# Grouped-query decode attention on one core: a shorter TensorE program with its prologue behind the loop, branch hints, and small ScalarE steps on GpSimd

## The chip, the cores and the metric

One core of a Trainium2 chip: TensorE (matrix products), VectorE, ScalarE, GpSimd, SyncE (which here issues most transfers) and 16 DMA engines that load from HBM into SBUF. The metric is the device time of one execution in microseconds, the median of several runs of the same program.

## The reference

One decode step for a batch of 2: layer norm, grouped-query attention over a cache of 32,768 keys and values for 8 key/value heads (32 query heads, 4 to each key/value head, 128 wide), an output projection, gated by a small two-layer block. Cut to what matters:

```python
xn = layernorm(x)                                   # x: [2, 1, 512]
q = (xn @ wq).reshape(B, 1, 32, 128).transpose(0, 2, 1, 3)
k, v = repeat(k_cache, 4, axis=1), repeat(v_cache, 4, axis=1)   # caches: [2, 8, 32768, 128]
p = softmax(einsum("bhqd,bhkd->bhqk", q, k) * 128 ** -0.5)
s = einsum("bhqk,bhkd->bhqd", p, v).reshape(B, 1, 4096) @ wo
x1 = xn + shifted(gelu(layernorm(xn) @ w1)) @ w2    # with one position, every shift gives zeros
g = silu(x1 + gelu(layernorm(x1) @ w3) @ w4)
out = x + s * g
```

All inputs are bfloat16. The caches are 268 of the 280.5 MB that are read.

## The kernel before

A *group* is one (batch, key/value head) pair; there are 16, each with 8.4 MB of K and 8.4 MB of V. The program is written out engine by engine, ordered by semaphores alone; `Queue` counts an engine's instructions, and `take` waits for a semaphore and lowers it.

- SyncE loads wq, w3, w4 and the first K (L214 to L217), then for each group K (L342) once half of the last group's scores are done (`s_half`), V (L331) once the last P·V is done (`s_pv`), for the last group in halves (L348, L336), and at the end wo in three parts (L354). K has three half-size slots in `kbuf`, V two in `vbuf`; wq lies in K's third slot.
- VectorE (loop at L406, two groups a turn) turns K in 16 blocks into tiles `T` (L416, four buffers), finds the peak of the scores (L399, L401, L426, L428 give `shift`), transposes the exponentials into `pt` (L432), forms row sums (L431) and their reciprocal (L436). Late in the next group it finishes the previous group's head: `on` (L385), `xm` and `oXs` (L389, L393).
- TensorE (loop at L468, a group a turn) makes the scores (L477), the sum of the peaks (L487), the softmax sum (L492, two fp32 products), P·V into four quadrants of `o` (L500); in the middle of the next group `head_oT` (L452, four fp32 products over `ob`) and `head_xp` (L462). After the loop it repeats the two heads for the last group and makes the output product with wo (L518, 128 products).
- ScalarE makes the exponentials (L374), and copies: `z`, the weights of the next group's scores (L360, four pieces), `ob` from `o` (L379), `oX` from `oXs` (L367).
- The prologue makes q (L287, L294) and the gate (L305, L317) while the first K is loading.

Both loops have `head_slot` 0: the loop's first instruction is placed at the start of a block in which the engine fetches its instructions. TensorE's prologue lies ahead of its loop in memory, the output product behind it.

Of the kernel before, what the change touches and what calls it, by code (L numbers as in the profile page):

```python
# [18 lines left out]
VT = 4  # L19
# [44 lines left out]

@with_exitstack
def kernel(
# [55 lines left out]
    rs = [sb(f"rs{i}", [128, 1], F32) for i in range(NPART)]  # L122
    sm = [sb(f"sm{i}", [128, rep], F32) for i in range(NPART)]
# [18 lines left out]
    sel_o = sb("sel_o", [128, VT, rep], F32)  # L142
    sel_h = sb("sel_h", [128, rep], F32)
# [7 lines left out]
    xn_bf = sb("xn_bf", [B, D], BF16)  # L151
    ln2_bf = sb("ln2_bf", [B, D], BF16)
    xT = sb("xT", [128, 2 * DK, B], BF16)
    q_sb = sb("q_sb", [128, B, Hq], BF16)
# [14 lines left out]
    S = bank("S", rep + NPART * 32)  # L169
# [19 lines left out]
    pe = Queue(nc.tensor, sem("s_pe"))  # L189
# [6 lines left out]
    t_d = sem("t_d")  # L196
# [15 lines left out]
    with tc.tile_critical(no_gpsimd_drain=True):  # L212
# [8 lines left out]
        e_x4z = po.op(lambda e: e.memset(x4_bf[:, :], 0.0))  # L221
        e_id0 = po.op(lambda e: e.memset(ident[:, :], 0.0))
# [6 lines left out]
        po.op(lambda e: e.memset(ob[:, :], 0.0), inc=(t_ob, 1))  # L229
# [4 lines left out]
        e_o0 = ve.op(lambda e: e.memset(o[:, :], 0.0))  # L234
        ve.op(lambda e: e.memset(pro[:, :], 0.0))
        e = ve.op(lambda e: e.tensor_copy(out=xf[:, :], in_=x_bf[:, :]), (d_x, 16))
# [15 lines left out]
        e_xnb = ve.op(lambda v: v.tensor_copy(out=xn_bf[:, :], in_=xn[:, :]), e_xn)  # L252
        e = layernorm(ln2, xn, "ln2", e_xn)
        e_lnb = ve.op(lambda v: v.tensor_copy(out=ln2_bf[:, :], in_=ln2[:, :]), e)
        for j in range(4):
# [5 lines left out]
            axis=AX.X, op=ALU.add))  # L261
        e_selh = ve.op(lambda v: v.tensor_reduce(
# [14 lines left out]
        treg = xp_b[:, :].bitcast(BF16)  # L277
        for s, (src, ev) in enumerate(((xn_bf, e_xnb), (ln2_bf, e_lnb))):
            for k in range(DK):
                c = (s * DK + k) * B  # L280
                e = pe.op(lambda t, c=c, src=src, k=k: t.transpose(
                    out=treg[:, c:c + B], in_=src[0:B, k::DK], identity=ident[0:B, 0:B]), ev, e_id)
        e_xT = ve.op(lambda v: v.tensor_copy(out=xT[:, :, :], in_=treg[:, 0:2 * DK * B].rearrange("p (k b) -> p k b", b=B)), e)
        for h in range(Hq):
            for k in range(DK):
                last = h == Hq - 1 and k == DK - 1
                e = pe.op(lambda t, h=h, k=k: t.matmul(  # L287
                    pro[:, h * B:(h + 1) * B], lhsT=wq3[:, k, h * Dh:(h + 1) * Dh], rhs=xT[:, k, :],
                    start=(k == 0), stop=(k == DK - 1)), e_xT, (d_wq, 16), inc=last)
        e_q = ve.op(lambda v: v.tensor_copy(out=q_sb[:, :, :], in_=pro[:, 0:Hq * B].rearrange("p (h b) -> p b h", b=B)), e)  # L290
# [10 lines left out]
        hT = sc[0]  # L301
        for f in range(FK):
            for k in range(DK):
                last = f == FK - 1 and k == DK - 1
                e = pe.op(lambda t, f=f, k=k: t.matmul(  # L305
                    hT[:, f * B:(f + 1) * B], lhsT=w3v[:, k, f::FK], rhs=xT[:, DK + k, :],
                    start=(k == 0), stop=(k == DK - 1)), (d_w3, 16), inc=last)
        e_hf = ve.op(lambda v: v.tensor_copy(out=hf[:, :], in_=hT[:, 0:FK * B]), e)
# [30 lines left out]
        for m in range(1, NG):  # L339
            base = m % 2  # L340
            if m < NG - 1:
                sp.op(lambda e, m=m, base=base: e.dma_start(  # L342
                    out=kbuf[:, base * SLOT:(base + NPART) * SLOT], in_=row_view(A_k_cache, *groups[m])),
                    (s_half, m), e_q, inc=(t_k[0], 16))
                nc.sync.sem_inc(t_k[1], 16)
            else:
                for i, h in enumerate(order(m)):
                    sp.op(lambda e, m=m, h=h, base=base: e.dma_start(  # L348
                        out=kbuf[:, (base + h) * SLOT:(base + h + 1) * SLOT],
                        in_=row_view(A_k_cache, *groups[m])[:, h * SLOT:(h + 1) * SLOT]),  # L350
                        (s_half, m), inc=(t_k[i], 16))
            load_v(m, (s_pv, m))
        for i, (a, c) in enumerate(wo_parts):
            sp.op(lambda e, a=a, c=c: e.dma_start(out=wo3[:, a:c, :], in_=wos[:, a:c, :]), (s_pv, NG - 1), inc=(d_wo[i], 16))  # L354


        def put_z(b, k):
            for j in range(4):
                c = (NR - 1) * rep + 32 * j
                ac.op(lambda v, j=j, c=c: v.copy(  # L360
                    out=z[32 * j:32 * j + 32, :, :, c:c + rep],
                    in_=qr[32 * j:32 * j + 32, :, :, b, k * rep:(k + 1) * rep]),
                    e_qr, e_z0, inc=(t_z, 1) if j == 3 else False)

        def keep_oX(m):
            b, k = groups[m]
            return ac.op(lambda v: v.copy(out=oX[:, k, :, b], in_=oXs[:, :]), (s_oX, m + 2))  # L367

        put_z(*groups[0])
        for m in range(NG):  # L370
            if m:
                keep_oX(m - 1)
            for i in range(NPART):
                ac.op(lambda v, i=i: v.activation(  # L374
                    out=ep[i][:, :], in_=sc[i][:, :], func=ACT.Exp, scale=inv_sqrt_dh, bias=shift[:, :], accum_out=rs[i][:, :]),
                    (s_shift, m + 1), e_tf if m == 0 else None, inc=(t_e, 1))
            if m < NG - 1:
                put_z(*groups[m + 1])
            ac.op(lambda v: v.copy(out=ob[:, :], in_=o[:, :]), (s_pv, m + 1), inc=(t_ob, 1))  # L379
        e_oX = keep_oX(NG - 1)  # L380
# [6 lines left out]
        def head_out():  # L387
# [4 lines left out]
            with nc.allow_low_precision(reason="three of the four terms are zero, the fourth is bf16"):  # L392
                nc.vector.tensor_reduce(out=oXs[:, :], in_=xm[:, :, :], axis=AX.X, op=ALU.add).then_inc(s_oX, 1)  # L393
# [12 lines left out]
        with nc.Fori(0, NG // 2, engines=[DVE], head_slot={DVE: 0}):  # L406
            for par in range(2):
                for i, h in enumerate(order(par)):
# [3 lines left out]
                    for r in range(NR):  # L412
                        n = i * NR + r
                        if n >= T_BUFS:
# [3 lines left out]
                            in_=kt[:, r * W:(r + 1) * W].rearrange("p (t b k) -> p t b k", b=NB, t=RT)).then_inc(t_T, 1)  # L418
                        if i == 1 and r == 3:
# [6 lines left out]
                nc.vector.tensor_reduce(out=top[:, :], in_=S[:, rep:], axis=AX.X, op=ALU.max).then_inc(t_d, 1)  # L426
                take(nc.vector, t_d)
                nc.vector.tensor_scalar_mul(out=shift[:, :], in0=top[:, :], scalar1=-inv_sqrt_dh).then_inc(s_shift, 1)  # L428
                for i, h in enumerate(order(par)):
                    take(nc.vector, t_e)  # L430
                    nc.vector.tensor_scalar_mul(out=sm[i][:, :], in0=sel_h[:, :], scalar1=rs[i][:, 0:1])  # L431
# [4 lines left out]
                nc.vector.reciprocal(out=rec[:, :], in_=S[:, 0:rep]).then_inc(t_oT, 1)  # L436
        head_on()
        head_out()
# [10 lines left out]
        def head_oT(first=None):  # L449
            take(nc.tensor, t_ob)  # L450
            for t in range(VT):
                ins = nc.tensor.matmul(  # L452
                    oT[:, :], lhsT=ob[:, t * Dh:(t + 1) * Dh], rhs=sel_o[:, t, :],
                    start=(t == 0), stop=(t == VT - 1))
                if t == 0 and first is not None:
                    ins.then_inc(first, 1)
            ins.then_inc(t_oT, 1)
# [9 lines left out]
        pe.wait(e_o0, e_ones, e_const, e_hf, e_tf)  # L467
        with nc.Fori(0, NG, engines=[PE], head_slot={PE: 0}):  # L468
            take(nc.tensor, t_z)
            for i in range(NPART):  # L470
                for r in range(NR):
# [3 lines left out]
                    for nb in range(NB):  # L475
                        for w in range(2):
# [3 lines left out]
                                stop=(r == NR - 1 and nb == NB - 1 and w == 1))  # L480
                    ins.then_inc(t_used, 1)
                    if i == 1 and r == 3:
                        head_xp()
                if i == 0:
                    head_oT(s_half)
            take(nc.tensor, t_mx)
            nc.tensor.matmul(  # L487
                S[:, rep:], lhsT=same_h[:, :], rhs=mxr[:, :, :].rearrange("p i r -> p (i r)"),
                start=True, stop=True).then_inc(t_top, 1)
            take(nc.tensor, t_pt, NPART)  # L490
            for i in range(NPART):
                ins = nc.tensor.matmul(S[:, 0:rep], lhsT=ones_f[:, :], rhs=sm[i][:, :], start=(i == 0), stop=(i == NPART - 1))  # L492
            ins.then_inc(t_S, 1)
# [13 lines left out]
        head_oT()  # L507
        head_xp()


        for i, (a, c) in enumerate(wo_parts):
            for k in range(a, c):
                pe.wait(e_s0, e_oX, (d_wo[i], 16))
                for r in range(NQ):
                    gr = k * NQ + r
                    for n in range(NQ):
                        col = r * D + n * QW
                        pe.op(lambda t, k=k, r=r, n=n, col=col, gr=gr: t.matmul(  # L518
                            pro[32 * n:32 * n + B, 0:QW], lhsT=oX[:, k, r, :], rhs=wo3[:, k, col:col + QW],
                            start=(gr == 0), stop=(gr == Hkv * NQ - 1), tile_position=(0, 32 * n)),  # L520
                            inc=(gr == Hkv * NQ - 1 and n == NQ - 1))
# [30 lines left out]
```

## Time and profile before

| | us |
|---|---|
| median of 3 runs | 659.79 (659.31 to 660.29) |
| the profiled execution | 659.97 |
| its span, first to last instruction | 657.6 |
| busy: TensorE / VectorE / ScalarE / GpSimd | 413.3 / 372.4 / 53.1 / 2.2 |
| DMA: 280.5 MB at a mean of 427 GB/s, share of 16 engines | 98.7% |

The profile lists, for one execution, each engine's work by source line, what ended its idle time, DMA queues with packets and bytes, and slices or windows of time with the share that 16 DMA engines were busy. A row such as "L416 DVE ... x8 [1.91 <-DVEq L396]" reads: eight instructions of line 416 on VectorE in a row, idle 1.91 us before them, ended by the engine's own queue at line 396 (`take`). Transfers of data are in queue q1 (from SyncE) and q10 (from ScalarE); packets of the kind "instruction" bring the engines' programs.

### The profile page before, as it was taken

The numbers are of one execution on the slowest core, as the hardware profiler recorded it, in microseconds if no ns is written. First come the engines' busy times: TensorE is split into PE (matmuls) and PEld (weight loads), VectorE is DVE, ScalarE is ACT, GpSimd is POOL, SyncE is SP. The second block draws the span as 40 slices with busy tenths as digits, with TensorE's granted clock in tenths as the row PEclk, the third lists the DMA queues.
The fourth block names the chain that finished last, engine by engine and source line by source line (L and its number), as shares of the span: only waits on it lengthen the run. The fifth ranks groups of instructions, "written<-read, shape, count | busy, mean of one in ns | idle before, by whom it ended". The sixth has DMA issues, their size and how long they took to land. (4 is left out here: it accounts for less than half of the span.)

```text
span 657.6 us, 7019 instructions
## 1 busy us (share of the span) xinstructions
PE 413.3 (63%) x2654; PEld 180.6 (27%) x2686; DVE 372.4 (57%) x530; ACT 53.1 (8%) x168; POOL 2.2 (0%) x11
## 2 busy tenths in 40 slices
PE   2528386564838756583865659476574947657965
PEld 2313132231313223131322313132232413213423
DVE  4238193663819367291945729184582918548760
ACT  1110101010010101001010100101010010100010
POOL 1000000000000000000000000000000000000000
PEclk9959787687978769797876979788697977869797
DMA  8999999999999999999999999999999999999995
GB/s 366 432 445 438 443 446 403 438 439 442 442 407 438 438 442 442 419 427 438 442 442 427 423 442 435 442 435 415 442 435 442 438 411 442 438 442 419 419 426 222
DMA packets 6460, 280.61 MB, mean 427 GB/s; under 512 B 682, under 2 KB 692, under 8 KB 1716
## 3 DMA queue, kind: packets, MB, share of 16 engines
q1 hardware_dynamic: 6408, 280.50, 98.7%
q8 instruction: 4, 0.07, 0.0%
q14 instruction: 4, 0.03, 0.0%
q10 hardware_dynamic: 44, 0.01, 0.0%
HBM read 280.50 MB, written 0.00 MB: 427 GB/s over the span
## 5 line engine op out<-in xcount | busy, mean ns | idle before, releaser
L416 DVE STREAM_TRANSPOSE T<-kbuf 128x1024 int32<-128x1024 int32 x256 | 292.8, 1210 | 177.4 <-DVEq L396 177.4
L477 PE MATMUL sc<-T,z 128*128 128x512 bf16 x992 | 270.8, 420 | 146.7 <-PEq L396 142.5
L477 PEld LDWEIGHTS sc<-T,z 128*128 128x128 bf16 x1024 | 99.7, 104 | 304.4 <-issue 221.4
L500 PE MATMUL o<-vbuf,pt 128*16 128x512 bf16 x1024 | 91.1, 535 | 0.0
L492 PE MATMUL S<-sm,ones_f 128*128 128x4 f32 x64 | 15.8, 352 | 53.6 <-PEq L396 53.6
L500 PEld LDWEIGHTS o<-vbuf,pt 128*16 128x16 bf16 x1024 | 30.5, 118 | 52.9 <-issue 45.1
L367 ACT COPY oX<-oXs 128x4 bf16<-128x4 bf16 x16 | 3.1, 196 | 375.8 <-DVE oXs L393 375.8
L399 DVE TENSOR_REDUCE mx<-sc 128x1 f32<-128x512 f32 x32 | 21.5, 672 | 15.7 <-DVEq L396 15.7
L492 PEld LDWEIGHTS S<-sm,ones_f 128*128 128x128 f32 x64 | 14.8, 322 | 55.3 <-issue 55.3
L374 ACT ACTIVATE ep<-sc,shift 128x512 bf16<-128x512 f32 x32 | 21.7, 683 | 77.1 <-DVE shift L428 77.1
L432 DVE STREAM_TRANSPOSE pt<-ep 128x512 bf16<-128x512 bf16 x32 | 22.6, 705 | 0.0
L487 PE MATMUL S<-mxr,same_h 128*128 128x64 f32 x32 | 6.5, 285 | 22.0 <-PEq L396 22.0
L452 PEld LDWEIGHTS oT<-sel_o,ob 128*128 128x128 f32 x136 | 17.7, 191 | 4.0 <-issue 1.3
L379 ACT COPY ob<-o 128x512 f32<-128x512 f32 x16 | 9.4, 586 | 115.0 <-PE o L500 115.0
L452 PE MATMUL oT<-sel_o,ob 128*128 128x4 f32 x136 | 16.2, 242 | 0.8 <-PEq L396 0.8
L431 DVE TENSOR_SCALAR sm<-sel_h,rs 128x4 f32<-128x4 f32 x32 | 6.7, 209 | 15.4 <-DVEq L396 15.4
L436 DVE RECIPROCAL rec<-S 128x4 f32<-128x4 f32 x16 | 2.9, 183 | 20.5 <-DVEq L396 20.5
L487 PEld LDWEIGHTS S<-mxr,same_h 128*128 128x128 f32 x32 | 4.8, 188 | 29.8 <-issue 29.8
L360 ACT COPY z<-qr 32x16 bf16<-32x16 bf16 x64 | 12.6, 197 | 3.9 <-issue 3.3
L401 DVE TENSOR_SCALAR mxr<-row_of,mx 128x32 f32<-128x32 f32 x32 | 7.7, 241 | 4.8 <-DVEq L396 0.3
L426 DVE TENSOR_REDUCE top<-S 128x1 f32<-128x64 f32 x16 | 3.6, 225 | 11.2 <-DVEq L396 11.2
L385 DVE TENSOR_TENSOR on<-oT,rec 128x4 bf16<-128x4 f32 x17 | 2.7, 156 | 7.9 <-DVEq L396 7.9
(73 smaller groups left out, 72.7 us busy)
## 6 DMA issues: line engine op xcount, KB each, us to landing
kbuf<-in_A_k_cache_dram SPq DMA_DIRECT2D x2, 4096.0 KB, 21.9
vbuf<-in_A_v_cache_dram SPq DMA_DIRECT2D x2, 4096.0 KB, 20.4
kbuf<-in_A_wq_dram SPq DMA_DIRECT2D x1, 4096.0 KB, 12.2
vbuf<-in_B_w_dram SPq DMA_DIRECT2D x2, 1792.0 KB, 18.6
kbuf<-in_A_wo_dram SPq DMA_DIRECT2D x1, 2048.0 KB, 29.5
kbuf<-in_A_wo_dram SPq DMA_DIRECT2D x1, 1536.0 KB, 32.8
kbuf<-in_A_wo_dram SPq DMA_DIRECT2D x1, 512.0 KB, 33.5
kbuf<-in_A_k_cache_dram SPq DMA_DIRECT2D x15, 27.6
```

The lines of the kernel that those rows point to most:

```text
L360: ac.op(lambda v, j=j, c=c: v.copy(out=z[32 * j:32 * j + 32, :, :, c:c + rep], in_=qr[32 * j:32 * j + 32, :, :, b, k * rep:(k + 1) * rep]) ...
L374: ac.op(lambda v, i=i: v.activation(out=ep[i][:, :], in_=sc[i][:, :], func=ACT.Exp, scale=inv_sqrt_dh, bias=shift[:, :], accum_out=rs[i][: ...
L379: ac.op(lambda v: v.copy(out=ob[:, :], in_=o[:, :]), (s_pv, m + 1), inc=(t_ob, 1))
L399: nc.vector.tensor_reduce(out=mx[:, i:i + 1], in_=sc[i][:, :], axis=AX.X, op=ALU.max).then_inc(t_d, 1)
L401: ins = nc.vector.tensor_scalar_mul(out=mxr[:, i, :], in0=row_of[:, :], scalar1=mx[:, i:i + 1])
L416: nc.vector.transpose(out=Ts[n % T_BUFS][:, :].rearrange("p (b t k) -> p t b k", b=NB, t=RT), in_=kt[:, r * W:(r + 1) * W].rearrange("p (t ...
L432: nc.vector.transpose(out=pt[h][:, :, :].rearrange("p r (t h) -> p t r h", h=rep), in_=ep[i][:, :].rearrange("p (t r h) -> p t r h", r=NR, ...
L452: ins = nc.tensor.matmul(oT[:, :], lhsT=ob[:, t * Dh:(t + 1) * Dh], rhs=sel_o[:, t, :], start=(t == 0), stop=(t == VT - 1))
L477: ins = nc.tensor.matmul(sc[i][:, :], lhsT=z[:, nb, w, zc:zc + 128], rhs=Tb[:, nb, :, w], start=(r == 0 and nb == 0 and w == 0), stop=(r = ...
L487: nc.tensor.matmul(S[:, rep:], lhsT=same_h[:, :], rhs=mxr[:, :, :].rearrange("p i r -> p (i r)"), start=True, stop=True).then_inc(t_top, 1)
L492: ins = nc.tensor.matmul(S[:, 0:rep], lhsT=ones_f[:, :], rhs=sm[i][:, :], start=(i == 0), stop=(i == NPART - 1))
L500: ins = nc.tensor.matmul(o[32 * j:32 * j + VT * rep, :], lhsT=pt[h][:, r, a * VT * rep:(a + 1) * VT * rep], rhs=vt[:, u * VT:(u + 1) * VT, ...
```

## The change

TensorE's program: the prologue is recorded and placed behind the loop. A register `turn` counts: at 0 the first branch goes to the prologue, at 1 to 16 to a group, then on to the output. The prologue computes q and the gate with xT as the weights and 448 to 512 columns of wq or w3 as the moving side, in four quadrants, and VectorE transposes the results: 32 and 16 products instead of 128 and 56. `head_oT` is one fp32 product instead of four, because VectorE now masks `o` and adds its four quarters (`head_ob`, in place of ScalarE's copy of `o`); the softmax sum is one product of 8 columns, added by VectorE. The output product starts ahead of the last `head_xp`. A branch hint stands ahead of the output product; VectorE's loop has a hint for its back edge instead of `head_slot`. GpSimd makes `z` (one masked product instead of four copies) and copies `oX`; the last `oX` is written by VectorE. SyncE releases `head_ob` with `t_o`, after each V issue.

```diff
-    pe = Queue(nc.tensor, sem("s_pe"))
+    pe = LateQueue(nc.tensor, sem("s_pe"))      # keeps what it is given until place()
...
+        for i in range(NPART):
             for k in range(DK):
+                for n in range(NQ):
+                    e = pe.op(lambda t, i=i, k=k, n=n: t.matmul(
+                        sc[i][32 * n:32 * n + B, :], lhsT=xT[:, k, :],
+                        rhs=wq3[:, k, :].rearrange("p (h n y) -> p h n y", n=NQ, y=32)[:, i * HH:(i + 1) * HH, n, :],
+                        start=(k == 0), stop=(k == DK - 1), tile_position=(0, 32 * n)), ...)
+            e = ve.op(lambda v, i=i: v.transpose(out=qT[:, i * 512:(i + 1) * 512], in_=sc[i][:, :]), e)
...
             load_v(m, (s_pv, m))
+            nc.sync.sem_inc(t_o, 1)
...
+        sp.wait((s_pv, NG))
+        nc.sync.sem_inc(t_o, 1)
...
-        def put_z(b, k):
-            for j in range(4):
-                c = (NR - 1) * rep + 32 * j
-                ac.op(lambda v, j=j, c=c: v.copy(
-                    out=z[32 * j:32 * j + 32, :, :, c:c + rep], ...
+        def put_z(m):
             b, k = groups[m]
+            po.op(lambda v: v.tensor_mul(out=z_cols,
+                in0=qr[:, :, :, b, k * rep:(k + 1) * rep].rearrange(...).broadcast_to([128, 2 * NB, 4, rep]),
+                in1=quad[:, :].unsqueeze(1).unsqueeze(3).broadcast_to([128, 2 * NB, 4, rep])),
+                e_qr, e_z0, e_quad, (s_shift, m) if m else None, inc=(t_z, 1))
...
-            ac.op(lambda v: v.copy(out=ob[:, :], in_=o[:, :]), (s_pv, m + 1), inc=(t_ob, 1))
...
+        def head_ob():
+            take(nc.vector, t_o)
+            nc.vector.tensor_mul(
+                out=ob[:, :].rearrange("p (t d) -> p t d", t=VT), in0=o[:, :].rearrange("p (t d) -> p t d", t=VT),
+                in1=row_t[:, :].unsqueeze(2).broadcast_to([128, VT, Dh])).then_inc(t_d, 1)
+            take(nc.vector, t_d)
+            nc.vector.tensor_reduce(
+                out=obm[:, :], in_=ob[:, :].rearrange("p (t d) -> p d t", t=VT), axis=AX.X, op=ALU.add).then_inc(t_ob, 1)
...
-        with nc.Fori(0, NG // 2, engines=[DVE], head_slot={DVE: 0}):
+        with nc.Fori(0, NG // 2, engines=[DVE], hint_back_edge=True):
...
+                        if i == 0 and r == 3:
+                            head_ob()
...
-            for t in range(VT):
-                ins = nc.tensor.matmul(
-                    oT[:, :], lhsT=ob[:, t * Dh:(t + 1) * Dh], rhs=sel_o[:, t, :],
-                    start=(t == 0), stop=(t == VT - 1))
+            nc.tensor.matmul(oT[:, :], lhsT=obm[:, :], rhs=sel_h[:, :], start=True, stop=True).then_inc(t_oT, 1)
...
-        with nc.Fori(0, NG, engines=[PE], head_slot={PE: 0}):
+        with nc.body("pe_turn", valid_engines=[PE]):
+            nc.br_ne(turn, 0, on_true="pe_groups", on_false="pe_prologue", engines=[PE])
+        with nc.body("pe_groups", valid_engines=[PE]):
...
+            nc.br("pe_next", engines=[PE])
+        with nc.body("pe_output", valid_engines=[PE]):
+            in_next_block = nc.tensor.mark_branch_hint_location()
+            head_oT()
+            for i, (a, c) in enumerate(wo_parts):
+                if i == 1:
+                    nc.tensor.br_ne(turn, 0, "pe_output_2", "pe_turn").branch_hint(in_next_block)
+                    nc.switch_bb("pe_output_2")
+                    head_xp()
...
+        with nc.body("pe_prologue", valid_engines=[PE]):
+            prologue.place()
...
+        with nc.body("pe_next", valid_engines=[PE]):
+            nc.regs_alu(turn, turn, 1, op=ALU.add)
+            nc.br_lt(turn, NG + 1, on_true="pe_turn", on_false="pe_output", engines=[PE])
```

## The prediction

> **What bounds the kernel now.** I read the page's slices first, then its DMA queues.
>
> ```profile
> GB/s 366 432 445 438 443 446 403 438 439 442 442 407 438 438 442 442 419 427 438 442 442 427 423 442 435 442 435 415 442 435 442 438 411 442 438 442 419 419 426 222
> ...
> q1 hardware_dynamic: 6408, 280.50, 98.7%
> q8 instruction: 4, 0.07, 0.0%
> q14 instruction: 4, 0.03, 0.0%
> ```
>
> The 16 DMA engines are busy for 98.7% of the span, so nothing that VectorE or TensorE does in the middle sets the time. The DMA view cut to 80:640 says the same more sharply, and names the one other thing that uses these engines:
>
> ```profile
> q1 hardware_dynamic: 4492, 242.62, 100.0%
> q14 instruction: 1, 0.01, 0.0%
> ```
>
> Instructions come through the same engines. Narrow windows of that view place the q8 packets at 19.1, 35.7 and 74.1 us and, by a window over the end, after 640; each takes its engine 0.9 us (5.0%, 4.9% and 4.6% of 16 engines over 1.2 us). The q14 packets stand at 35.8, 41.5 and 146.9, 0.3 us each. I read q8 as TensorE's: its packets come as TensorE is in the prologue, enters the loop, ends the first turn, and nears the last matmul. Through the next 14 turns there is none.
>
> A lump on one engine is never made up, since every engine always has its next load queued. The windows at the end show it (columns: span, busy us and count by engine, clock, DMA share, GB/s):
>
> ```profile
> 649.00:649.50 0.50, 0.00 (x0) 0.00 (x0) 0.24 (x2) 0.00 (x0) 0.00 (x0) 0.52 0.90 369
> 649.50:650.00 0.50, 0.07 (x6) 0.10 (x10) 0.10 (x1) 0.20 (x1) 0.00 (x0) 0.50 0.32 131
> 650.00:650.50 0.50, 0.50 (x24) 0.50 (x27) 0.00 (x0) 0.00 (x0) 0.00 (x0) 0.50 0.24 98
> 650.50:651.00 0.50, 0.50 (x32) 0.50 (x24) 0.00 (x0) 0.00 (x0) 0.00 (x0) 0.50 0.14 57
> 651.00:651.50 0.50, 0.50 (x32) 0.50 (x24) 0.00 (x0) 0.00 (x0) 0.00 (x0) 0.50 0.04 16
> ```
>
> Most engines finish at 649.5; about four go on, the last to about 651.3. After 649.5 are left (0.32 + 0.24 + 0.14 + 0.04) x 0.5 us x 16 = 5.9 engine-us. Shared evenly they would end 0.4 us later, at 649.9: the stragglers make every load land up to 1.4 us late.
>
> The last group then runs as a chain. Its rows in the timeline, and the chain of waits behind them:
>
> ```profile
> 612.81 9.24 DVE L416 STREAM_TRANSPOSE T<-kbuf 128x1024 int32<-128x1024 int32 x8 [1.91 <-DVEq L396]
> ...
> 616.33 0.59 ACT L379 COPY ob<-o 128x512 f32<-128x512 f32 x1 [7.22 <-PE o L500]
> ...
> 622.62 4.62 DVE L416 STREAM_TRANSPOSE T<-kbuf 128x1024 int32<-128x1024 int32 x4 [0.57 <-DVEq L396]
> ...
> 639.23 0.98 PE L492 MATMUL S<-sm,ones_f 128*128 128x4 f32 x4 [3.35 <-PEq L396]
> ...
> 646.51 0.59 ACT L379 COPY ob<-o 128x512 f32<-128x512 f32 x1 [8.47 <-PE o L500]
> ```
>
> ```profile
> 648.72 0.24 PE xp L462 x4
> 648.96 0.97 issue
> 649.93 3.16 PE pro L518 x126
> 653.09 0.02 issue
> 653.12 0.30 DVE sg L442
> ```
>
> Both halves of the last K make VectorE wait (1.91 and 0.57 us): 622.62 is set by DMA. From there all is compute: P·V ends at 646.45, and 6.64 us of ob, oT, on, xp, oXs, oX and the output product follow, to 653.09.
>
> **The change, part by part.** The sum is made on the profiled execution: 659.97 us, that is a span of 657.6 and 2.4 around it, 0.2 above the median of 659.79.
>
> *Instruction fetches.* Moving the prologue behind the loop puts the loop in the part of the program that is there before the first q8 packet; 299 fewer instructions leave fewer pieces to bring. I count one of TensorE's fetches left in the stream (the start jumps past the loop into the prologue, which brings what lies behind it) out of three, and one of VectorE's two, since it now falls into its loop without a jump; ScalarE loses 96 copies and perhaps its packet at 146.9. The straggler now is about 1.8 us behind 649.5 and carries by its size more than one lump. One lump costs between its own 0.9 us and the 1.4 us that even sharing would save; I take 1.2, by the middle. Gain 1.8 - 1.2 = 0.6. Bounds: 0 (as many lumps as now) and 1.6 (none left: 1.4 and the lumps' own 3.7 engine-us over 16).
>
> By the Trainium skill (Runtime: NRT & Kernel Launch, "Instruction fetch mechanics") a sequencer holds two 16 KiB pieces, and a taken branch to a third stalls for a DMA fetch; the same section gives TensorE 128 KiB. The trace fits the larger figure: no q8 packet in 80:640 though each turn branched back. By the smaller one the new loop, whose end now stands behind the prologue in a third piece, would fetch each turn; that is the second rival.
>
> *head_ob.* ScalarE's ob copy (0.59) becomes two VectorE operations inside the transposes of the first half. Nearest rows: the 2x512 f32 add from PSUM 0.68, the 512-wide max L399 0.67, with 0.15 between dependent ones: 1.5 us. Below, 1.2 (two 0.53 passes, as the 2x512 L247); above, 3.0, if the strided reduce and the broadcast double. In turns 0 to 13 it is hidden: VectorE waits 11.7 us for each K, and V's load is issued 5.9 us before K's lands (114.28 against a first transpose at 120.23), so DMA doesn't run dry while V is issued 1.0 us later. What is queued behind the new wait for t_o is the second four transposes; t_o comes from SP behind V's issue. In group 14 the 1.5 us, less 0.5 for the S product (two passes of 0.25 instead of four), put the end of P·V at 617.3; SP's two issues take 0.85, so t_o comes at 618.2, while VectorE is ready at 612.81 + 4.62 = 617.43. Wait 0.8, work 1.5: the first half ends at 624.35 instead of 622.05, and the second starts 1.7 after 622.62. The last S gives back 0.5. Sum at the end of P·V: +1.2.
>
> *The tail.* Semaphore through SP and multiply 0.3 + 0.68, reduce 0.15 + 0.67, oT 0.14 + 0.3 (one product of two passes, was eight passes in 1.03): oT at +2.25. Then 64 of the 128 output products run while VectorE makes on (64 x 0.0247 = 1.6; their oX are long done), head_xp 0.3, 48 products 1.2, with xm and the reduce, now straight into oX, beside them, and 16 products 0.4 with starts: +5.45 instead of 6.64, so -1.2. The wo parts, 646.7 to 651.7 now, are there in time.
>
> *The rest costs nothing, by this cover.* GpSimd's z and oX: no row; between its 128x128 memset, 0.2, and ten times that; cover, the 15 us from shift to the next K. Without it, its own length per turn. Two more branches a turn on TensorE, under its wait for the first transposed tile (7.8 us before L477 in the third turn). The new prologue: 32 and 16 wide products instead of 128 and 56 narrow ones. At L500's rate, which has the same four quadrants (64 in 5.8 us), 2.9 + 1.5 us against 3.6 + 3.5; at L317's 0.39 each 18.7, 11.6 more. I take L500's. Cover: z is ready at 34.1 and needed at 44.4, V's first load is issued at 28.6 with K in the queue until 43; at worst 1.3 us come through. Two more memsets and reductions on VectorE (about 2 us) lie ahead of the wait for wq (4.7 us). SP's 17 added instructions start no transfer.
>
> Sum: -0.6 + 1.2 - 1.2 = -0.6, with rounding of the parts +0.1: 659.97 - 0.5 = 659.5; against the median, **659.3**.
>
> **The rivals.**
> *All fetches gone from the stream.* Even sharing then, gain 1.5 to 1.6: 659.79 - 1.55 = 658.2. For it: no q8 packet stands before 19.1, so what is loaded ahead is not small. Against: the program still is more than what was there at 19.1.
> *A fetch every turn.* If the piece that ends the loop isn't kept, 15 turns x 0.9 us on one engine's ring are 13.4, less the 1.8 it lags now: 671.4; spread over all engines, 659.8 or so. For it: the loop spans more pieces. Against: none in 80:640 now. It decides from the third turn on.
> *head_ob becomes the bound.* At 3.0 us: t_o at 619.7, the first half ends at 627.3, 3.0 later than forecast, the tail 1.5 more: 659.3 + 4.5 = 663.8, slower than before. Decides above 2.0 us for the pair. For it: a stride of 512 bytes in the reduce and a broadcast operand, with no row. Against: L399, L320.
> *It doesn't do what it says.* As many lumps as now: 659.9.
>
> **How the numbers follow.** Forecast 0.47, all fetches gone 0.20, fetch every turn 0.09, head_ob 0.14, no effect 0.10. The range reaches from 657.6 (all gone, and head_ob at 1.2) to 663.0, which leaves out the fetch every turn, the upper half of the head_ob case and a little below; the forecast's own is 658.5 to 660.4. A difference under 0.2% (1.3 us) can't be told from none here. Faster: 0.22, all gone and a sliver of the forecast; slower 0.23, the two slow rivals; same 0.55.
>
> **What would show it.** q8 packets in the stream one instead of three, and none in 80:640; the share after the bulk's end shorter than 1.8 us. Rows for ob and obm of 0.7 us each; VectorE waiting for t_o in the last group alone; the end of P·V about 1 us later against K's landing and the output product's end 5.5 after it. Wrong: rows of 1.5 for obm, q8 packets all along, or a gap ahead of the output product.

## The result, and the profile after

The changed kernel takes 661.80 us (median of 8 runs, 660.85 to 662.16) against 659.76 us for the kernel before (8 runs, 658.97 to 660.29): a ratio of 1.0029, 95% interval 1.0018 to 1.0040. It is slower by about 2 us, where 659.3 was forecast: inside the range, on the other side of no change. The profiled execution took 662.16 us with a span of 660.0.

The page after, in the same rows as before, and the DMA view cut to 80:640:

```profile
GB/s 361 442 438 441 445 437 421 417 445 441 445 433 417 425 445 441 441 429 422 429 445 441 441 421 429 429 445 441 437 425 429 429 445 441 433 425 419 435 414 167
...
q1 hardware_dynamic: 6408, 280.50, 98.3%
q8 instruction: 2, 0.03, 0.0%
q14 instruction: 4, 0.03, 0.0%
```

```profile
q1 hardware_dynamic: 4455, 242.35, 99.9%
q14 instruction: 2, 0.02, 0.0%
```

The q8 packets are two instead of four (at 4.1 us, among the first loads, and at 653.1), and none stands in 80:640. The loads profit: by the DMA records the last half of K lands at 621.85 instead of 622.37 us, the last part of wo at 651.16 instead of 651.68. So 0.5 us is gained up to there. All of the loss lies behind, in the last group and the tail. VectorE in the timeline of the last group (start, busy time, engine, line, operation, in brackets the idle time ahead):

```profile
612.26 4.62 DVE L481 STREAM_TRANSPOSE T<-kbuf 128x1024 int32<-128x1024 int32 x4 [0.46 <-DVEq L461]
618.61 0.69 DVE L442 TENSOR_TENSOR ob<-o,row_t 128x512 f32<-128x512 f32 x1 [1.72 <-DVEq L461]
619.45 1.05 DVE L446 TENSOR_REDUCE obm<-ob 128x128 f32<-128x512 f32 x1
620.42 5.74 DVE L481 STREAM_TRANSPOSE T<-kbuf 128x1024 int32<-128x1024 int32 x5
```

Read the brackets first. Before, the second half of K made VectorE wait 0.57 us and was taken up as it landed. Now VectorE itself waits 1.72 us for `t_o` and works 1.81 us (618.61 to 620.42) on `head_ob`, and the second half's transposes start at 624.95, 3.1 us after its landing. The smaller S product gives 0.4 back; P·V ends at 648.33 instead of 646.45. The chain that ended last, from there:

```profile
650.53 0.36 PE oT L526 x2
650.89 1.66 PE pro L599 x64
652.55 0.20 PE xp L531 x4
652.75 1.59 PE pro L599 x54
654.34 1.14 issue
655.47 0.35 PE pro L599 x10
```

"issue" is time in which TensorE waited for nothing that the profile shows: 1.14 us in the midst of 64 equal products. TensorE ends 7.48 us after P·V, where it was 6.61 before and 5.45 forecast.

The sum of this profile against the one of before: landing -0.52, P·V's end against the landing +2.40, tail +0.87, what lies behind the last product -0.40 (4.17 us instead of 4.56): +2.35, which is the difference of the two spans, 657.62 and 659.97.

### The profile page after: what moved, and what is told of

Read it like the earlier page. It is cut to its first block, busy times and chain, and to the rows that moved or that the text cites. A ratio compares the mean times of both kernels' runs of the same rounds, so it can differ in the third digit from the quotient of the medians.

```text
span 660.0 us, 6591 instructions
## 1 busy us (share of the span) xinstructions
PE 423.8 (64%) x2412; PEld 151.6 (23%) x2412; DVE 404.0 (61%) x571; ACT 29.6 (4%) x72; POOL 9.7 (1%) x42
## 5 line engine op out<-in xcount | busy, mean ns | idle before, releaser
L550 PE MATMUL sc<-T,z 128*128 128x512 bf16 x1024 | 295.8, 424 | 137.1 <-PEq L461 128.2
L550 PEld LDWEIGHTS sc<-T,z 128*128 128x128 bf16 x1024 | 92.6, 103 | 325.8 <-issue 268.0
L566 PE MATMUL S<-sm,ones_f 128*128 128x8 f32 x32 | 9.0, 354 | 51.8 <-PEq L461 51.8
L566 PEld LDWEIGHTS S<-sm,ones_f 128*128 128x128 f32 x32 | 7.9, 307 | 53.5 <-issue 53.5
L446 DVE TENSOR_REDUCE obm<-ob 128x128 f32<-128x512 f32 x17 | 17.7, 1040 | 2.5
L442 DVE TENSOR_TENSOR ob<-o,row_t 128x512 f32<-128x512 f32 x17 | 11.2, 656 | 7.6 <-DVEq L461 7.6
L526 PEld LDWEIGHTS oT<-sel_h,obm 128*128 128x128 f32 x34 | 6.3, 188 | 5.4 <-issue 2.7
L329 PE MATMUL sc<-kbuf,xT 128*2 128x512 bf16 x32 | 3.6, 627 | 5.5 <-DMA kbuf<-in_A_wq_dram 5.5
L366 PE MATMUL sc<-vbuf,h_bf 128*2 128x512 bf16 x14 | 4.9, 522 | 2.4 <-DVE h_bf L363 2.4
L420 POOL TENSOR_TENSOR z<-qr,quad 128x64 bf16<-128x64 bf16 x16 | 4.7, 294 | 107.6 <-DVE shift L495 90.4
## 6 DMA issues: line engine op xcount, KB each, us to landing
vbuf<-in_A_v_cache_dram SPq DMA_DIRECT2D x2, 4096.0 KB, 18.6
```

What stands on the lines that cost most here:

```text
L442: nc.vector.tensor_mul(out=ob[:, :].rearrange("p (t d) -> p t d", t=VT), in0=o[:, :].rearrange("p (t d) -> p t d", t=VT), in1=row_t[:, :]. ...
L446: nc.vector.tensor_reduce(out=obm[:, :], in_=ob[:, :].rearrange("p (t d) -> p d t", t=VT), axis=AX.X, op=ALU.add).then_inc(t_ob, 1)
L550: ins = nc.tensor.matmul(sc[i][:, :], lhsT=z[:, nb, w, zc:zc + 128], rhs=Tb[:, nb, :, w], start=(r == 0 and nb == 0 and w == 0), stop=(r = ...
L566: nc.tensor.matmul(S[:, 0:NPART * rep], lhsT=ones_f[:, :], rhs=sm[:, :, :].rearrange("p i h -> p (i h)"), start=True, stop=True).then_inc( ...
```

## The experiments

Theory A: two things cost, `head_ob` on VectorE (in the last group, and as a later issue of V in every group) and the branch hint (the gap). Each kernel ran beside the kernel before on the same chip: 659.36 us in the first batch (the first four below), 659.81 in the second (head_ob off VectorE, head_ob alone, the prologue ahead, the second profile of before), 659.97 in the third.

### The hint taken out

```diff
-            in_next_block = nc.tensor.mark_branch_hint_location()
...
-                    nc.tensor.br_ne(turn, 0, "pe_output_2", "pe_turn").branch_hint(in_next_block)
+                    nc.tensor.br_ne(turn, 0, "pe_output_2", "pe_turn")
```

> Theory A (the hint puts off the fetch of the program's last piece until the hinted branch): without it a q8 packet comes as TensorE enters the output, about 647 to 652, and the 1.14 us gap ahead of the last ten output products is gone. It shares an engine with wo, whose last part is then up to 1.4 us later, 651.2 to 652.6, still ahead of its use at about 654. Time 661.8 - 1.1 = 660.7. Rival B (the gap is a wait for the last part of wo or for the last oX): the gap stays, 661.8.

660.44 us (11 runs, 659.25 to 661.55), ratio 1.0014 [1.0005, 1.0023]. TensorE at the end:

```profile
651.31 1.77 PE L598 MATMUL pro<-kbuf,oX 128*2 128x128 bf16 x64
653.01 0.27 PE L531 MATMUL xp<-on,sel_r 128*128 128x4 bf16 x4
653.21 1.84 PE L598 MATMUL pro<-kbuf,oX 128*2 128x128 bf16 x64
```

The 64 products behind `xp` are one row: no gap. The q8 packet comes at 652.3 us, 2.3 us ahead of the 119th of the 128 products; in the changed kernel it came at 653.1, 1.2 us ahead of the place where TensorE stopped, which is in front of the same product. By the two ratios, 1.0029 and 1.0014, about half of the loss is the hint's; their intervals overlap a little.

### head_ob two transposes later, ob laid out the other way, and all three

```diff
-                        if i == 0 and r == 3:
+                        if i == 0 and r == 5:
                             head_ob()
```

> head_ob after six transposes instead of four. Theory A (in the last group VectorE waits 1.72 us for t_o, and that wait is on the chain that ends last): the wait is gone, the first half ends at 623.3 instead of 625.0, still behind the landing of the second half of K at 621.9, so all of it counts: 661.8 - 1.7 = 660.1. Rival C (the loss lies in the steady turns or in DMA, VectorE's wait is cover): 661.8.

661.78 us (5 runs, 660.59 to 662.11; the profiled one is the fastest), ratio 1.0040 [1.0026, 1.0054]: a miss. The wait for `t_o` is gone from the profile and P·V ends at 646.80, yet nothing is won, because the chain has another link at the end:

```profile
618.68 33.10 DMA kbuf<-in_A_wo_dram
651.78 0.14 issue
651.92 0.28 PE pro L599 x6
652.19 1.81 issue
654.00 0.35 PE pro L599 x10
```

TensorE now gets ahead of the last part of wo (landed at 651.78), and then runs into the same gap, 1.81 us long. What is saved ahead of the gap comes back in it.

```diff
-                out=ob[:, :].rearrange("p (t d) -> p t d", t=VT), in0=o[:, :].rearrange("p (t d) -> p t d", t=VT),
+                out=ob[:, :].rearrange("p (d t) -> p t d", t=VT), in0=o[:, :].rearrange("p (t d) -> p t d", t=VT),
...
-                out=obm[:, :], in_=ob[:, :].rearrange("p (t d) -> p d t", t=VT), ...
+                out=obm[:, :], in_=ob[:, :].rearrange("p (d t) -> p d t", t=VT), ...
```

> ob written quarter by quarter interleaved, so that the reduction reads it in order. Theory A (the stride of 512 bytes makes the reduction take 1.04 instead of the 0.67 of a 512-wide max): 0.67 each; 0.37 less in group 14 (by t_o), in group 15 and in the tail: 661.8 - 1.1 = 660.7. Rival D (the length is that of 128 separate sums of four, or the interleaved write makes the product as much longer): row sums as before, 661.8.

660.94 us (5 runs), ratio 1.0035 [1.0021, 1.0048]. The groups of both kernels (count, then busy us and mean ns of one), first the changed kernel, then this one:

```profile
L446 DVE TENSOR_REDUCE obm<-ob 128x128 f32<-128x512 f32 x17 | 17.7, 1040 | 2.5
L442 DVE TENSOR_TENSOR ob<-o,row_t 128x512 f32<-128x512 f32 x17 | 11.2, 656 | 7.6 <-DVEq L461 7.6
```

```profile
L442 DVE TENSOR_TENSOR ob<-o,row_t 128x512 f32<-128x512 f32 x17 | 17.4, 1026 | 5.8 <-DVEq L461 5.8
L446 DVE TENSOR_REDUCE obm<-ob 128x128 f32<-128x512 f32 x17 | 11.7, 686 | 2.5
```

The strided side costs some 0.35 to 0.37 us, whether it is read (1040 against 686 ns) or written (1026 against 656). The pair stays at 1.7 us.

> The three edits together. Theory A: -1.1 (no gap), -1.7 (no wait for t_o), -0.75 (two reductions on the chain, group 14's no longer being there): 661.8 - 3.5 = 658.3, under the kernel before (659.8) by 1.5. If only B, C or D hold in one place, that term is missing.

All three edits together: 661.05 us (6 runs, 658.76 to 661.78), ratio 1.0025 [1.0009, 1.0040], a miss again. There is no gap and no wait for `t_o`, but VectorE waits elsewhere:

```profile
618.85 2.37 DVE L481 STREAM_TRANSPOSE T<-kbuf 128x1024 int32<-128x1024 int32 x2 [1.09 <-DVEq L461]
621.15 1.02 DVE L442 TENSOR_TENSOR ob<-o,row_t 128x512 f32<-128x512 f32 x1
622.31 0.69 DVE L446 TENSOR_REDUCE obm<-ob 128x128 f32<-128x512 f32 x1
```

`T` has four buffers, and TensorE frees none while it is in P·V, which ended at 617.69. So VectorE stops after four transposes here, whatever stands behind them, and only the work of `head_ob` itself is left to remove.

### head_ob off VectorE

The copy of `o` goes back to ScalarE, and GpSimd masks it and adds the quarters, in groups 0 to 14; for the last group, whose head follows P·V directly, VectorE keeps `head_ob`. No hint. GpSimd's three operations, with the names shortened:

```diff
+            if m < NG - 1:
+                e_ob[m] = ac.op(lambda v: v.copy(out=ob[:, :], in_=o[:, :]), (s_pv, m + 1))
...
+        def put_obm(m):
+            e = po.op(lambda v: v.tensor_mul(out=ob4, in0=ob4, in1=row_t_broadcast), e_ob[m], e_row)
+            e = po.op(lambda v: v.tensor_add(out=ob[:, 0:2 * Dh], in0=ob[:, 0:2 * Dh], in1=ob[:, 2 * Dh:]), e)
+            po.op(lambda v: v.tensor_add(out=obm[:, :], in0=ob[:, 0:Dh], in1=ob[:, Dh:2 * Dh]), e, inc=(t_ob, 1))
...
-                        if i == 0 and r == 3:
-                            head_ob()
```

> The changed kernel without the branch hint, and in the loop ScalarE copies o again and GpSimd masks and adds the quarters; VectorE does it for the last group alone. Theory A (VectorE's 1.7 to 1.9 us inside the first half, and the wait ahead of it, are on the chain of the last group, and push every V issue back): the second half of the last group starts within 0.6 us of K's landing, P.V ends about 23.7 us after that landing (24.1 in the kernel before, 26.5 in the changed one), V is issued 1.3 us earlier in each turn. Time 2.0 under the kernel without the hint, about 1 under the kernel before: ratio to before 0.9985. Rival C (the loss lies in the program's order, the fetches or GpSimd): as the kernel without the hint, ratio 1.0014 or more.

658.22 us (10 runs, 657.93 to 658.57), ratio 0.9980 [0.9970, 0.9989]: faster than both kernels. Its timeline where the changed kernel waited:

```profile
615.35 0.59 ACT L416 COPY ob<-o 128x512 f32<-128x512 f32 x1 [7.61 <-PE o L584]
616.01 1.04 POOL L430 TENSOR_TENSOR ob<-ob,row_t 128x512 f32<-128x512 f32 x1 [9.38 <-ACT ob L416]
617.13 0.74 POOL L433 TENSOR_TENSOR ob<-ob 128x256 f32<-128x256 f32 x1
617.95 0.46 POOL L434 TENSOR_TENSOR obm<-ob 128x128 f32<-128x128 f32 x1
...
622.04 1.25 DVE L492 STREAM_TRANSPOSE T<-kbuf 128x1024 int32<-128x1024 int32 x1 [0.72 <-DVEq L472]
```

GpSimd is done at 618.4, and VectorE waits 0.72 us for the second half of K, which landed at 621.80: DMA sets the pace again. P·V ends at 645.51, 2.8 us sooner than in the changed kernel.

### head_ob alone, in the kernel before

The kernel before, in which only `head_ob` goes to VectorE, with `t_o` and the single product for oT:

```diff
-            ac.op(lambda v: v.copy(out=ob[:, :], in_=o[:, :]), (s_pv, m + 1), inc=(t_ob, 1))
...
             load_v(m, (s_pv, m))
+            nc.sync.sem_inc(t_o, 1)
...
+                        if i == 0 and r == 3:
+                            head_ob()
```

> The kernel before with one part of the change alone: head_ob on VectorE, one fp32 product in head_oT. Theory A: the last group's first half ends 2 to 3 us later, the tail's mask and sum take 0.75 more than copy and four products: 2.7 to 3.5 over before, ratio 1.004 to 1.0053. Rival C: the tail's 0.75 alone, ratio 1.001.

663.89 us (6 runs, 662.77 to 665.52), ratio 1.0064 [1.0048, 1.0079]: more than was expected. The DMA view of this kernel in 80:640, to be read against the row of the kernel before in the prediction (4492 packets, 242.62 MB):

```profile
q1 hardware_dynamic: 4405, 241.50, 100.0%
```

In the same 560 us it moved 1.12 MB less, 2.6 us of loading at 433 GB/s; the share of busy time says 100.0% and shows nothing of it. K's landings fall behind those of before by 0.9 us at 120 us, 2.1 at 199 us and 3.3 at the last. V's second issue stands at 77.48 instead of 74.52. By the DMA records that is some 1.5 us before the first of the 16 DMA engines was through with K, where the kernel before left about 4: from 79.0 to 79.5 us the engines are busy for 0.55 of the time, and full in the kernel before. Most of the loss hides in packets that take longer than others of their size: from 74 to 640 us, 71 of 32 or 64 KB took over 0.2 us longer than usual, most of them just behind an issue of V, 36 us of engine time together; in the kernel before it was 6 packets and 1.7 us.

So `head_ob` costs some 4 us here (0.0064 of 659.81), the most of it on loads that land later (3.3 us in this profile), the rest in the last group. The changed kernel left at least some 2.5 us in groups 2 to 14 of its first profile and 3 of its second. Its landings kept what they had gained in the first; in the second they lost 0.4 us between 544 and 583 us, with no long packet behind an issue of V to explain it. The margin is thin: in the profile of the kernel without its hint, with a lead of some 2.5 us, the landings lost 0.5 us between 274 and 313 us, and three packets behind V's issue at 269.86 took 2.9 to 4.0 us where 2.4 is usual.

### The prologue ahead of the loop

The changed kernel without its hint, with the prologue ahead of an ordinary loop and the output product behind it:

```diff
-    pe = LateQueue(nc.tensor, sem("s_pe"))
+    pe = Queue(nc.tensor, sem("s_pe"))
...
-        with nc.body("pe_groups", valid_engines=[PE]):
+        with nc.Fori(0, NG, engines=[PE], head_slot={PE: 0}):
```

> The changed kernel without the branch hint, with the prologue ahead of TensorE's loop in memory again and the loop's head at the start of a fetch block; all else stays. Theory A (where the prologue stands is worth little): two q8 packets in the stream, about 35 and 74 us, instead of one at 4; wo lands 0 to 0.5 later; ratio to before 1.0014 to 1.002. Rival F (the new order itself, with its branches and its fetch as the first data come, is what costs): ratio 1.0005 or less.

659.77 us (12 runs, 658.31 to 660.95), ratio 0.9998 [0.9988, 1.0008]. By A it should have been 1.0014 or more; F is the nearer. The two profiles differ in the clock. The windows 644:648 of the kernel without its hint, then of this one:

```profile
644.00:648.00 4.00, 4.00 (x44) 1.36 (x40) 0.00 (x0) 0.00 (x0) 0.00 (x0) 0.50 1.02 421
```

```profile
644.00:648.00 4.00, 2.74 (x40) 0.84 (x32) 0.91 (x2) 0.00 (x0) 0.00 (x0) 0.83 1.02 421
```

P·V of the last group took 6.39 us at a granted clock of 0.50, and 5.81 where the clock came back during it. The wait for `t_o` differs too, 1.64 us against 0.49. The loads are a small part, 622.40 against 622.05 for the last K, and neither has a gap. The order was then tried on the kernel with GpSimd:

> The copy of o back on ScalarE and the sums on GpSimd, no hint, and the prologue ahead of the loop in memory, with an ordinary loop around it. Theory A (the late values' load and the stall of the hint are the whole loss, the order of the pieces costs nothing): the same as the kernel with the prologue behind the loop, 0.998 of the kernel before, within 0.0008. Rival F (the order with the prologue behind the loop costs some 0.15% by itself, as 0.9998 against 1.0014 hinted): 0.9965 or less. A third outcome: with the prologue first the fetches of instructions fall into the second and third groups again and the loads land 0.3 us later: 0.9985.

658.00 us (7 runs, 657.77 to 658.09), ratio 0.9971 [0.9960, 0.9982], against 0.9980 [0.9970, 0.9989] with the prologue behind the loop. It falls between A and F, and the intervals overlap. Whether the order costs anything stays open; by these two ratios it would be 0.09%, by the pair without GpSimd 0.16%. It beats both kernels too.

### The hint put back, and two second profiles

> The copy of o back on ScalarE and the sums on GpSimd, the hint kept: beside the kernel without it in the batch before, the hint is the only difference. Theory A: the hint puts off the last fetch, so that a gap of 1 to 1.8 us with no release stands between the output's products, and the ratio is 0.9995 (0.998 and 1.0 us). Rival: without the wait for o the fetch has time, the gap is gone and the ratio is 0.998.

660.10 us (11 runs), ratio 0.9999 [0.9990, 1.0009], against 0.9980 [0.9970, 0.9989] without the hint; these two intervals just don't overlap. The chain:

```profile
650.15 1.66 PE pro L608 x41
651.80 2.11 issue
653.91 0.50 PE pro L608 x8
```

> The changed kernel once more, for a second profile. Theory A: the gap of some 1 us between the output's products again, a wait of 1.5 to 1.9 us for o ahead of the first product of head_ob, and the values' load issued 4 to 5.5 us ahead of the end of the keys' load in every group. Rival: the gap was an accident of the one profiled execution and is not there.

One run, 661.8 us. The chain has a gap of 1.86 us. The wait for `t_o`, however, is half of the first profile's, which this expectation missed:

```profile
617.90 0.69 DVE L442 TENSOR_TENSOR ob<-o,row_t 128x512 f32<-128x512 f32 x1 [0.87 <-DVEq L461]
618.74 1.05 DVE L446 TENSOR_REDUCE obm<-ob 128x128 f32<-128x512 f32 x1
619.70 3.49 DVE L481 STREAM_TRANSPOSE T<-kbuf 128x1024 int32<-128x1024 int32 x3
```

> The kernel before once more, for a second profile: how far the landings of the last K (622.4) and of wo (651.7), the end of P.V (646.5) and the wait behind it move from run to run. If the first profile is typical, each within 0.3; the packets of instructions at the same places (q8 at 19, 36, 74).

660.11 us, with q8 packets at 18.6, 33.1, 74.0 and 652.3, and the last K and wo at 622.42 and 651.72. Against the second profile of the changed kernel (621.93 and 651.17), the gain on the loads is 0.5 us again.

## Why the prediction was wrong

*Instruction fetches: the count was right, the gain fits but is not isolated.* Of three TensorE packets in the stream one is left, none stands in 80:640; 0.6 us was priced, 0.5 measured in both pairs of profiles. The rivals of all fetches gone (1.6) and of a fetch in every turn are out. But the count alone doesn't set the landing: three kernels made from this one (no hint, `head_ob` later, all three), with the same single packet, landed the last K at 622.40 to 622.67, no sooner than before, and the two with two packets in the stream (the prologue ahead) at 622.05 and 622.01.

*head_ob: the mechanism was right, two terms were too small.* P·V of group 14 was put at 617.3 and came at 617.56 and 616.85. The pair was priced at 1.5 us, with the reduce taken for the contiguous row L399, 0.67; its stride of 512 bytes made it 1.04, and the pair with its handover 1.8. The wait for `t_o` was priced at 0.8 and measured 1.72 and 0.87. So P·V ended 2.4 and 1.6 us later against K's landing (the second profiles: 23.64 us before, 25.25 after), where +1.2 was written. The rival in which `head_ob` becomes the bound decides "above 2.0 us for the pair"; it came near that, and its stride was the cause, but the 3.0 us were not reached.

*The tail: this step failed.* "+5.45 instead of 6.64, so -1.2" priced the branch hint at nothing. The prediction's own sign of being wrong, "a gap ahead of the output product", came, though in the midst of it. In both profiles the tail grew, to 7.48 and 8.26 us, by 0.87 and 1.18 against the profiles of before. The gap is 1.14 and 1.86 of it. In five profiles with the hint (these two, head_ob later, ob the other way, the hint put back) a gap of 1.05 to 2.11 us with no release stands among the last products, each time between the 118th and the 119th of the 128, and TensorE goes on 1.3 to 1.5 us after the last q8 packet has landed. In the five made from it without the hint, TensorE stops among these products for no more than 0.2 us except until a part of wo has landed. Two of these five say little, since with the prologue ahead of the loop the last q8 packet lands behind the last product; three are left as the test.

Undoing the hint is worth 0.0015 of the time on the changed kernel and 0.0019 on the one with GpSimd, 1.0 and 1.25 us, by ratios from different batches. The trace's records place the hint at 646.32, the branch that it belongs to at 651.71 and the last q8 packet at 653.14, with 0.96 us of transfer, and TensorE goes on at 655.47. Without the hint the packet comes 0.8 to 1.5 us behind the first output product (three kernels), with it 2.3 to 2.4 us behind it, and 4.7 us in the kernel with GpSimd, where TensorE waited for wo in between. So the hint costs this time, and the gap fits a wait for that packet. How the hint makes the packet late stays open. A fetch held back until the hinted branch has run would fit four profiles, with the packet 1.4 to 1.7 us behind the branch; but with the hint put back on the kernel with GpSimd the branch ran at 647.59 and the packet came at 651.63, 4.0 us later.

By the Trainium skill (Runtime: NRT & Kernel Launch, "Instruction fetch mechanics") a sequencer fetches its next page while it executes the current one, and that is mostly hidden. The kernel without the hint agrees: its last packet made no gap. The kernels with it do not.

Without the gap the tail is 6.34 and 6.40 us, still 0.9 over the forecast: 0.3 is the pair again, 0.3 is a sum of mine (the terms written there make 5.75, not 5.45), and the rest the pace of the output products, 0.026 to 0.029 us in the first profile instead of 0.0247.

*V issued later.* "DMA doesn't run dry while V is issued 1.0 us later" held for this kernel, though by less than I thought: I measured the lead to K's landing, which is that of the slowest DMA engine. The fastest was done 2 us sooner.

So the time was 661.8 instead of 659.3: by the two pairs of profiles +0.4 to +1.2 for `head_ob`, +2.1 to +2.4 for the tail, -0.4 behind it.

## What to carry to other kernels

A hint for a branch, or any edit to the program's flow, can cost at its far end, as here: look for "issue" among equal instructions with no release, and where the last instruction packet falls. Work taken off a slack engine is paid on the engine that the last stretch waits for; GpSimd, idle 99% of the span, took over the same 1.7 us of VectorE in 2.4 us of its own, behind ScalarE's copy of 0.59 us, and that kernel was the faster one. Where loads bound the kernel, the lead of each issue is measured to the first DMA engine that runs out of work, not to the landing.

## What was unexpected of the hardware

The granted clock of TensorE falls to 0.50 in stretches, most of them of 3.4, 6.8 or 10.2 us, that shift from one execution to the next: P·V of the last group met one at 640.8 to 647.6 in the first profile after, at 639.2 to 646.0 in the second. The last group's P·V takes 5.3 to 6.5 us by that, and the wait for `t_o` behind the P·V of group 14 was 1.72 us in the one profile and 0.87 in the other. By the Trainium skill (TensorE: Matmul & The Clock Gate, "Part 1: The HAM clock gate (the "warmup" mystery)") the gate counts in free-running windows of 3.4 us; those stretches here are one, two or three of them long.

The spread of the runs seems to follow what sets the end. The two kernels with GpSimd and no hint, whose last products wait for wo to land and then meet no gap, lie within 0.6 and 0.3 us; the others, which end on a chain of compute or have the gap, spread over 1.1 to 3.0 us.
